# One PSUM bank per output row: product laid, rectified in place, y accumulated on it

## The chip, the cores and the metric

The kernel runs on one core of one Trainium2 chip. The metric is device time in microseconds (us). The kernel before was recorded at 440.18 us (median of 3 runs, 438.61 to 440.63). All times compared below are of fast runs unless a line says otherwise (a run counts as slow when it is over 1.5% above the fastest of the same kernel in its call).

## The reference

```python
scores = q @ k.T / sqrt(64), causal, window of 64 keys        # 8 batches, 8 heads, 576 rows
x = softmax(scores) @ v                                       # [8, 576, 512]
X = rfft(x, axis=1)[:, :64]                                   # 64 modes
Y = X * (w_r + i w_i)        # a 512 x 512 complex matrix for each mode
y = irfft(Y, n=576, axis=1)
u = x + y
out = u + relu(u @ w_ch)
```

The weights are 64 x 2 matrices of 512 x 512 in float32: 162 MB are read from HBM in all. `u @ w_ch` is computed as `x @ w_ch` (called Z here) plus the inverse transform of `Y @ w_ch`.

## The kernel before

There are three stages. The attention stage ends near 145 us; TensorE, ACT and DVE share it, and GpSimd issues the loads of weights as buffers come free. The mode stage follows the weight stream: mode after mode, 32 small matmuls each. Modes 0 to 47 (the 96 "early" rows of the spectrum) are folded into Z while the last 16 modes stream in. The tail starts when the last weight lands: the 32 "late" rows (modes 48 to 63) are transposed and multiplied with `w_ch` ("turn", once for each four batches), then 36 output row tiles are made. A row tile is 128 rows of one batch, or for `t = NT - 1` a pair of 64-row remainders of two batches.

The tail before, with two PSUM banks for each row (`psc` for the channel product, `psu` for y):

```python
def group(h, todo, folds, ...):                 # four rows at a time
    for b, t in todo:                           # Z into psc by an identity matmul
        nc.tensor.matmul(out=psc, lhsT=ident_r, rhs=channel_out(...), start=True, stop=False)
    for b, t, pair, psc in ts:                  # late rows, 32 of 128 contraction rows
        nc.tensor.matmul(out=psc, lhsT=trigL[pp, ...], rhs=Ywl[h][pp, :], start=False, stop=True)
    for i, (b, t, pair, psc) in enumerate(ts):
        fold = i in folds                       # x by a matmul, for about half of the rows
        ...                                     # if fold: psu = x_sb
        nc.tensor.matmul(out=psu, lhsT=trigI[...], rhs=Yb[...], ...)        # y
        nc.scalar.activation(out=r, in_=psc, func=Relu)
        if fold: nc.vector.tensor_tensor(out=ot, in0=psu, in1=r, op=add)
        else:    nc.vector.tensor_tensor(out=ot, in0=psu, in1=x_sb[...], op=add)
                 nc.gpsimd.tensor_tensor(out=ot, in0=ot, in1=r, op=add)
        nc.sync.dma_start(out=out[...], in_=ot)
```

A mode's matmuls, real and imaginary in turn for each of four output blocks `e`, and the eviction of eight modes at once by DVE and ACT:

```python
for e in range(NC):
    for c in range(NC): matmul(psy[:, m % MG, e, :], wr[...], XQ[...])
    if e == 0: between()
    for c in range(NC): matmul(psy[:, m % MG, e, :], wi[...], XQ[...])
...
if m % MG == MG - 1:
    for ri in range(2): evac(YT or YTl, psy, ri)     # DVE, then ACT
```

The softmax here doesn't subtract the row's maximum and nothing guards it: scores larger than these inputs give would overflow.

## Time and profile before

| | before |
|---|---|
| runs | 438.61, 440.18, 440.63 us |
| span of the profiled run | 438.7 us (that run: 440.46 us) |
| last imaginary matmuls start | 391.91 us |
| first late row | 397.60 us |
| last result in SBUF | 432.10 us |
| busy in the span: PE, DVE, ACT, POOL | 76%, 44%, 34%, 26% |

The times in the table are read from the list of instructions in order of time (start us, us, engine, line, operation, out<-in, count). Busy shares over the whole span say little here: they average an attention stage, a mode stage, and the tail. The prediction below shows the lines and how they were read.

This is ACT in the attention stage, in order of time (start us, us, engine, line, operation, out<-in, count):

```profile
51.70 1.74 ACT L58 COPY kT<-pst 128x768 bf16<-128x768 bf16 x2
53.33 1.09 ACT L292 ACTIVATE et<-pss 128x512 bf16<-128x512 f32 x2
```

### The profile page before, as it was taken

What the parts mean: (1) busy time and instruction counts of PE and PEld (TensorE: products, weight loads), DVE (VectorE), ACT (ScalarE), POOL (GpSimd) and SP (SyncE); (2) the same over time, 40 slices, a digit from 0 to 9 for tenths busy, and PEclk for the clock granted to TensorE, in tenths of its full rate; (3) what the DMA queues carried; (4) which work ended last, traced back from release to release, by engine and by line L of the source; (5) the groups of instructions that cost most, each with busy time, mean ns of one, the idle gap of its engine ahead of it and who ended that gap; (6) DMA issues with size and microseconds to landing.
All of it is one profiled execution on the core that took longest, in us unless ns stands there. A gap on an engine that the chain in (4) does not pass through costs nothing. (4 is left out here: it accounts for less than half of the span.)

```text
span 438.7 us, 11675 instructions
## 1 busy us (share of the span) xinstructions
PE 333.5 (76%) x5152; PEld 226.8 (52%) x5152; DVE 191.1 (44%) x384; ACT 147.4 (34%) x261; POOL 112.1 (26%) x188
## 2 busy tenths in 40 slices
PE   6999999989988864222388888986458666989991
PEld 2465666656654763112266676764335344555550
DVE  5465766666754004028522232222133433336772
ACT  4476866767753001001022232322001010105561
POOL 7131322231022232121122122221021212105473
PEclk9999999999998555555567898689585675899998
DMA  7999999999999999999999999999999999942685
GB/s 143 211 214 213 212 212 214 211 214 214 214 213 198 214 213 259 214 213 213 214 214 212 214 214 213 216 211 214 214 213 214 214 213 213 214 97 109 235 314 207
DMA packets 30643, 91.98 MB, mean 210 GB/s; under 512 B 3072, under 2 KB 3072, under 8 KB 30592
## 3 DMA queue, kind: packets, MB, share of 16 engines
q0 software_dynamic: 25344, 81.80, 93.6%
q1 hardware_dynamic: 5248, 9.44, 6.0%
q8 instruction: 40, 0.66, 0.5%
q14 instruction: 11, 0.09, 0.1%
HBM read 162.53 MB, written 9.44 MB: 392 GB/s over the span
## 5 line engine op out<-in xcount | busy, mean ns | idle before, releaser
L511 PE MATMUL psy<-XQ,wt 128*128 128x16 bf16 x880 | 54.9, 191 | 49.3 <-DMA wt<-in_moe_w_i_dram 47.9
L506 PE MATMUL psy<-XQ,wt 128*128 128x16 bf16 x912 | 57.2, 191 | 27.7 <-DMA wt<-in_moe_w_r_dram 27.1
L511 PEld LDWEIGHTS <-wt 128*128 128x128 bf16 x880 | 42.8, 104 | 59.9 <-DMA wt<-in_moe_w_i_dram 55.9
L506 PEld LDWEIGHTS <-wt 128*128 128x128 bf16 x912 | 43.1, 103 | 38.1 <-DMA wt<-in_moe_w_r_dram 34.5
L117 POOL DMA_DIRECT2D wt<-in_moe_w_i_dram x55 | 29.4, 535 | 125.9 <-PE psy L511 59.6
L541 DVE CAST xT<-pxt 128x512 fp32r<-128x512 bf16 x36 | 23.2, 686 | 64.9 <-PE pxt L538 64.9
L544 PE MATMUL psz<-wch,xT 128*128 128x512 f32 x144 | 48.8, 489 | 0.1
L117 POOL DMA_DIRECT2D wt<-in_moe_w_r_dram x57 | 30.7, 538 | 63.7 <-DMA wt<-in_moe_w_r_dram 35.3
L546 ACT CAST Z<-psz 128x512 fp32r<-128x512 f32 x36 | 21.1, 587 | 72.3 <-PE psz L544 72.3
L292 ACT ACTIVATE et<-pss 128x512 bf16<-128x512 f32 x72 | 39.2, 599 | 12.6 <-PE pss L286 12.5
L662 DVE TENSOR_TENSOR Z<-pse,Z 128x512 fp32r<-128x512 f32 x36 | 23.7, 688 | 33.6 <-PE pse L642 33.6
L310 PE MATMUL pso<-vt,et 128*64 128x65 bf16 (+1 forms) x576 | 32.6, 204 | 4.1 <-DVE x_sb L318 4.0
L544 PEld LDWEIGHTS psz<-wch,xT 128*128 128x128 f32 x144 | 31.9, 234 | 6.6 <-issue 0.2
L310 PEld LDWEIGHTS <-et 128*64 128x64 bf16 (+1 forms) x576 | 22.3, 109 | 15.6 <-issue 7.6
L751 POOL TENSOR_TENSOR ot<-ot,r 128x512 f32<-128x512 f32 x18 | 22.8, 1286 | 29.1 <-ACT Yb L58 24.0
L318 DVE TENSOR_TENSOR x_sb<-pso,rcp 128x640 bf16<-128x640 f32 x32 | 26.3, 822 | 0.9
L59 DVE CAST YT<-psy 128x256 fp32r<-128x256 f32 x6 | 2.5, 421 | 47.8 <-PE psy L511 47.8
L744 ACT ACTIVATE r<-psc 128x512 f32<-128x512 f32 x36 | 19.0, 601 | 10.3 <-PE psc L729 9.7
L267 PE MATMUL pss<-band,ident_bf 64*64 64x512 bf16 x160 | 20.6, 391 | 1.6 <-ACT et L292 1.6
L59 DVE COPY vT<-pst 128x768 bf16<-128x768 bf16 x16 | 15.3, 958 | 13.4 <-PE pst L213 13.4
L642 PE MATMUL pse<-yw,trigI 96*128 96x512 f32 x40 | 19.9, 566 | 0.0
L656 ACT CAST yw<-psw 96x512 fp32r<-96x512 f32 x8 | 4.7, 583 | 44.8 <-PE psw L653 44.8
(160 smaller groups left out, 532.5 us busy)
## 6 DMA issues: line engine op xcount, KB each, us to landing
wt<-in_moe_w_r_dram POOLq DMA_DIRECT2D x57, 512.0 KB, 19.1
wt<-in_moe_w_i_dram POOLq DMA_DIRECT2D x55, 512.0 KB, 19.1
out_dram<-ot SPq DMA_DIRECT2D x32, 256.0 KB, 2.2
rk<-in_k_dram POOLq DMA_DIRECT2D x8, 576.0 KB, 10.0
rq<-in_q_dram POOLq DMA_DIRECT2D x8, 576.0 KB, 13.8
rv<-in_v_dram POOLq DMA_DIRECT2D x8, 576.0 KB, 12.6
kT<-in_moe_w_i_dram POOLq DMA_DIRECT2D x2, 512.0 KB, 8.2
qT<-in_moe_w_r_dram POOLq DMA_DIRECT2D x2, 512.0 KB, 9.9
```

Of the source, the lines that this page charges most:

```text
L117: nc.gpsimd.dma_start(out=wt, in_=src[m].rearrange("(p c) e -> p c e", c=NC))
L267: nc.tensor.matmul(out=pss[(2 * w + hh) % 3][64 * half:64 * half + 64, :], lhsT=ident_bf[pp, pp], rhs=view(band[pp], 128 * half, [[0, WIN ...
L292: nc.scalar.activation(out=et[:, hh, :], in_=pss[(2 * w + hh) % 3], func=ACT_F.Exp, scale=EX_SCALE)
L310: nc.tensor.matmul(out=pso[po, hh, (i // 2) * VW:(i // 2) * VW + D + 1], lhsT=et[pk, hh, col:col + 64], rhs=vt[pk, 1 - f % 2, 2 * hh + g / ...
L318: nc.vector.tensor_tensor(out=view(x_sb, b * NT * DM + g * D, [[4 * D, 2], [DM, NT], [1, D]]), in0=view(pso, 0, [[512, 2], [VW, NT], [1, D]]),
L506: nc.tensor.matmul(out=psy[:, m % MG, e, :], lhsT=wr[:, c, ee], rhs=XQ[:, c, :, 1:3, m], start=(c == 0), stop=(m == 0 and c == NC - 1))
L511: nc.tensor.matmul(out=psy[:, m % MG, e, :], lhsT=wi[:, c, ee], rhs=XQ[:, c, :, 0:2, m], start=False, stop=(c == NC - 1))
L541: nc.vector.tensor_copy(out=xT, in_=pst)
L544: nc.tensor.matmul(out=psz, lhsT=xT[:, c, :], rhs=wch[:, c, :], start=(c == 0), stop=(c == NC - 1))
L546: nc.scalar.copy(out=channel_out(i), in_=psz)
L662: nc.vector.tensor_tensor(out=channel_out(i), in0=ps, in1=channel_out(i), op=ALU.add)
L751: nc.gpsimd.tensor_tensor(out=ot, in0=ot, in1=r, op=ALU.add)
```

## The change

The intent: a row keeps one PSUM bank. The identity matmul lays Z, the late rows are added, ACT rectifies the bank in place, y is accumulated on the rectified value, and one DVE add with x gives the result. GpSimd's adds and the x matmuls go. So that one table serves, late rows are placed by batch at partitions 96 to 127 of zero-padded tiles (`Ywm`, `Yb`), by GpSimd copies. The last mode gets its own bank: all its real matmuls, and the first four products, run before its imaginary weight lands. For the pair rows, x of the second batch is copied to partitions 64 to 127 of the first one's tile.

```diff
-    trigL = late2.tile([128, S + 64], FP32R, name="trigL")
...
-        if m % MG == 0:
+        if m % MG == 0 or m == NM - 1:
             psy = ps_y.tile([128, MG, NC, 2 * B], FP32, name="psy")
...                                     # in the building of the table trigI
-                    nc.vector.tensor_scalar(out=trigL[:, 576:640], ...)
+                for b in range(0, B, 2):
+                    nc.scalar.copy(out=x_sb[64:128, b, NT - 1, :], in_=x_sb[0:64, b + 1, NT - 1, :])
...                                     # last mode
+            for e in range(NC):
+                for c in range(NC):
+                    real(e, c)
+            between()                   # [z_row(i) for i in range(NR)] + [idle(6)]
             for c in range(NC):
+                for e in range(NC):
+                    imag(e, c)
...                                     # tail, NR = 4 and two more banks, LA = 2
+    def l_row(i):
+            nc.tensor.matmul(out=banks[i], lhsT=trigI[:, tr:tr + 128], rhs=Ywm[bb % NM2], start=False, ...)
+        nc.scalar.activation(out=banks[i], in_=banks[i], func=ACT_F.Relu)
+    def u_row(i):
+            nc.tensor.matmul(out=banks[i], lhsT=trigI[:, tr:tr + 128], rhs=Yb[bb // 2][:, bb % 2, :], start=False, ...)
+        nc.vector.tensor_tensor(out=ot, in0=banks.pop(i), in1=x_sb[...], op=ALU.add)
+        nc.sync.dma_start(...)
+        for i in range(len(order) + LA):
+            if i < len(order):
+                if i >= NR: z_row(i)
+                l_row(i)
+            if i >= LA: u_row(i - LA)
```

More of the change, by code (lines that the diff above doesn't have):

```diff
@@ L476 @@
     trigI = late2.tile([128, S + 128], FP32R, name="trigI")
-    trigL = late2.tile([128, S + 64], FP32R, name="trigL")
     Z0 = late2.tile([128, len(tiles), DM], FP32R, name="Z0")
-    p2d = ExitStack()
+    p2d = ctx.enter_context(ExitStack())
     ps_a = p2d.enter_context(tc.tile_pool(name="ps_a", bufs=1, space=PSUM, reuse_waits="tile"))
@@ L500, in mode, with real, imag @@
         wr, wi = wtiles.pop((m, 0)), wtiles.pop((m, 1), None)
-        if m % MG == 0:
+        if m % MG == 0 or m == NM - 1:
             psy = ps_y.tile([128, MG, NC, 2 * B], FP32, name="psy")
-        for e in range(NC):
-            ee = slice(128 * e, 128 * e + 128)
-            for c in range(NC):
-                nc.tensor.matmul(out=psy[:, m % MG, e, :], lhsT=wr[:, c, ee],
-                                 rhs=XQ[:, c, :, 1:3, m], start=(c == 0), stop=(m == 0 and c == NC - 1))
-            if e == 0:
-                between()
-            for c in range(NC if m else 0):
-                nc.tensor.matmul(out=psy[:, m % MG, e, :], lhsT=wi[:, c, ee],
-                                 rhs=XQ[:, c, :, 0:2, m], start=False, stop=(c == NC - 1))
+        def real(e, c):
+            nc.tensor.matmul(out=psy[:, m % MG, e, :], lhsT=wr[:, c, 128 * e:128 * e + 128],
+                             rhs=XQ[:, c, :, 1:3, m], start=(c == 0 and (m < NM - 1 or e == 0)),
+                             stop=(m == 0 and c == NC - 1), skip_group_check=True)
+        def imag(e, c):
+            nc.tensor.matmul(out=psy[:, m % MG, e, :], lhsT=wi[:, c, 128 * e:128 * e + 128],
+                             rhs=XQ[:, c, :, 0:2, m], start=False, stop=(c == NC - 1),
+                             skip_group_check=True)
+        if m < NM - 1:
+            for e in range(NC):
+                for c in range(NC):
+                    real(e, c)
+                if e == 0:
+                    between()
+                for c in range(NC if m else 0):
+                    imag(e, c)
+        else:
+            for e in range(NC):
+                for c in range(NC):
+                    real(e, c)
+            between()
+            for c in range(NC):
+                for e in range(NC):
+                    imag(e, c)
         while nw < NLOAD:
@@ L519, in mode @@
             nw += 1
-        if m % MG == MG - 1:
+        if m % MG == MG - 1 or m == NM - 2:
             g = m // MG
+            m0 = m % MG if m == NM - 1 else 0
+            n1 = m % MG + 1 - m0
             dst, n, g = (YT, E0, g) if g < L0 else (YTl, 128 - E0, g - L0)
-            for ri in range(2):
-                evac(view(dst, g * 2 * MG + ri * MG, [[B * n, NC], [n, B], [1, MG]]),
-                     view(psy, ri, [[2 * B, NC], [2, B], [NC * 2 * B, MG]]), ri)
+            if m < NM - 1:
+                for ri in range(2):
+                    evac(view(dst, g * 2 * MG + ri * MG, [[B * n, NC], [n, B], [1, n1]]),
+                         view(psy, ri, [[2 * B, NC], [2, B], [NC * 2 * B, n1]]), ri)
+            else:
+                evac(view(dst, g * 2 * MG + m0, [[B * n, NC], [n, B], [MG, 2]]),
+                     view(psy, m0 * NC * 2 * B, [[2 * B, NC], [2, B], [1, 2]]), False)
     with ExitStack() as p2a:
@@ L582, in floor @@
                         return f
-                    f32 = floor(32, pcol, "f32")
-                    f64 = floor(64, pcol, "f64")
-                    lcol, odd, even = col("lcol"), col("odd"), col("even")
-                    nc.vector.scalar_tensor_tensor(out=lcol, in0=f32, scalar=-32.0, in1=pcol,
-                                                   op0=ALU.mult, op1=ALU.add)
-                    nc.vector.tensor_single_scalar(out=lcol, in_=lcol, scalar=float(E0), op=ALU.add)
-                    nc.vector.scalar_tensor_tensor(out=odd, in0=f64, scalar=-2.0, in1=f32,
-                                                   op0=ALU.mult, op1=ALU.add)
-                    nc.vector.tensor_scalar(out=even, in0=odd, scalar1=-1.0, scalar2=1.0,
-                                            op0=ALU.mult, op1=ALU.add)
-                    for tab, row in ((trigI, pcol), (trigL, lcol)):
+                    for tab, row in ((trigI, pcol),):
                         fa, fb = floor(2 * MG, row, "fa"), floor(MG, row, "fb")
@@ L617 @@
                             nc.vector.tensor_scalar(out=tis, in0=tis, scalar1=coefs, scalar2=None, op0=ALU.mult)
-                            o2 = 576 if tab is trigI else 512
+                            o2 = 576
                             for c0, c1, o in ((0, SW, i * SW),) if i < 3 else ((0, 80, 432), (80, SW, o2)):
@@ L625 @@
                                             scalar2=None, op0=ALU.mult)
-                    nc.vector.tensor_scalar(out=trigL[:, 576:640], in0=trigL[:, 512:576], scalar1=odd,
-                                            scalar2=None, op0=ALU.mult)
-                    nc.vector.tensor_scalar(out=trigL[:, 512:576], in0=trigL[:, 512:576], scalar1=even,
-                                            scalar2=None, op0=ALU.mult)
+                for b in range(0, B, 2):
+                    nc.scalar.copy(out=x_sb[64:128, b, NT - 1, :], in_=x_sb[0:64, b + 1, NT - 1, :])
     yw = wmid.tile([128, 2, DM], FP32R, name="yw", tag="wm")
@@ L643, in early_rows, with z_row @@
                              start=start and r0 == 0, stop=stop and r0 + n == 128)
+    p3 = ctx.enter_context(ExitStack())
+    NM2 = 3
+    ywmp = p3.enter_context(tc.tile_pool(name="ywmp", bufs=1, side="right", reuse_waits="tile"))
+    Ywm = [ywmp.tile([128, DM], FP32R, name=f"Ywm{i}") for i in range(NM2)]
+    for t_ in Ywm:
+        nc.vector.tensor_scalar(out=t_[:E0], in0=trigI[:E0, 0:DM], scalar1=0.0, scalar2=None,
+                                op0=ALU.mult)
+    NR = 4
+    ps_e = p3.enter_context(tc.tile_pool(name="ps_e", bufs=NR, side="right", space=PSUM, reuse_waits="tile"))
+    order = []
+    for b in range(0, B, 2):
+        order += [(b, t) for t in range(NT - 1)] + [(b + 1, 0), (b, NT - 1)]
+        order += [(b + 1, t) for t in range(1, NT - 1)]
+    banks = {}
+    def z_row(i):
+        if i % (NR + 2) < NR:
+            banks[i] = ps_e.tile([128, DM], FP32, name="row", tag="pse")
+        else:
+            banks[i] = ps_f.tile([128, DM], FP32, name="rowf")
+        nc.tensor.matmul(out=banks[i], lhsT=ident_r, rhs=channel_out(tiles.index(order[i])),
+                         start=True, stop=False, skip_group_check=True)
     with ExitStack() as p2c:
-        ps_e = p2c.enter_context(tc.tile_pool(name="ps_e", bufs=3, space=PSUM, reuse_waits="tile"))
         def spectrum(b):
@@ L668, in idle @@
         def idle(n):
-            psd = ps_e.tile([128, DM], FP32, name="psd", tag="pse")
+            psd = ps_a.tile([128, DM], FP32, name="psd", tag="psa")
             for _ in range(n):
@@ L683 @@
             for m in range(L0 * MG, NM):
-                mode(m, lambda: some(1, m))
                 if m < NM - 1:
+                    mode(m, lambda: some(1, m))
                     some(2 if m % 8 != 7 else 1, m)
@@ L688 @@
                     assert not work
-                    idle(4)
+                    mode(m, lambda: [z_row(i) for i in range(NR)] + [idle(6)])
     p2b.close()
-    p2d.close()
     wl.close()
-    with ExitStack() as p3:
-        yp = p3.enter_context(tc.tile_pool(name="yp", bufs=1, reuse_waits="tile"))
-        tp = p3.enter_context(tc.tile_pool(name="tp", bufs=5, reuse_waits="tile"))
-        op = p3.enter_context(tc.tile_pool(name="op", bufs=11, reuse_waits="tile"))
-        ps_u = p3.enter_context(tc.tile_pool(name="ps_u", bufs=4, space=PSUM, reuse_waits="tile"))
-        ps_c = p3.enter_context(tc.tile_pool(name="ps_c", bufs=4, space=PSUM, reuse_waits="tile"))
-        R = 128 - E0
-        def turn(h):
-            psa = ps_u.tile([128, NC, 128], FP32R, name="psl", tag="psu")
-            psw = ps_c.tile([128, DM], FP32, name="pslw", tag="psc")
-            yl = [view(YTl, (e * B + 4 * h) * R, [[1, 128]]) for e in range(NC)]
-            for e in range(NC):
-                nc.tensor.transpose(out=psa[:, e, :], in_=yl[e], identity=ident_r)
-            for e in range(NC):
-                nc.tensor.matmul(out=psw, lhsT=yl[e], rhs=wch[:, e, :],
-                                 start=(e == 0), stop=(e == NC - 1))
-            for bb in range(4):
-                evac(Yb[2 * h + bb // 2][E0:128, bb % 2, :],
-                     psa[R * bb:R * bb + R].rearrange("p c e -> p (c e)"), bb == 3)
-                if bb == 2:
-                    nc.scalar.copy(out=Ywl[h], in_=psw)
-        def group(h, todo, folds, between=lambda: None):
-            ts = []
-            for b, t in todo:
-                psc = ps_c.tile([128, DM], FP32, name="psc", tag="psc")
-                nc.tensor.matmul(out=psc, lhsT=ident_r, rhs=channel_out(tiles.index((b, t))),
-                                 start=True, stop=False)
-                ts.append((b, t, t == NT - 1, psc))
-            between()
-            for b, t, pair, psc in ts:
-                pp = slice(R * (b - 4 * h), R * (b - 4 * h) + (2 * R if pair else R))
-                nc.tensor.matmul(out=psc, lhsT=trigL[pp, 128 * t:128 * t + 128], rhs=Ywl[h][pp, :],
-                                 start=False, stop=True)
-            for i, (b, t, pair, psc) in enumerate(ts):
-                fold = i in folds
-                psu = ps_u.tile([128, DM], FP32, name="psu", tag="psu")
-                if fold:
-                    for bb, r0, n in parts_of(b, t):
-                        nc.tensor.matmul(out=psu[r0:r0 + n, :], lhsT=ident_bf[:n, :n],
-                                         rhs=view(x_sb[:n], (bb * NT + t) * DM, [[1, DM]]),
-                                         start=True, stop=False)
-                for bb, r0, n in parts_of(b, t):
-                    tr = 128 * t + (64 - r0 if pair else 0)
-                    nc.tensor.matmul(out=psu, lhsT=trigI[:, tr:tr + 128], rhs=Yb[bb // 2][:, bb % 2, :],
-                                     start=not fold, stop=(r0 + n == 128))
-                r = tp.tile([128, DM], FP32, name="r")
-                nc.scalar.activation(out=r, in_=psc, func=ACT_F.Relu)
-                ot = op.tile([128, DM], FP32, name="ot")
-                if fold:
-                    nc.vector.tensor_tensor(out=ot, in0=psu, in1=r, op=ALU.add)
-                else:
-                    nc.vector.tensor_tensor(out=ot, in0=psu,
-                                            in1=view(x_sb, (b * NT + t) * DM, [[1, DM]]), op=ALU.add)
-                    nc.gpsimd.tensor_tensor(out=ot, in0=ot, in1=r, op=ALU.add)
-                for bb, r0, n in parts_of(b, t):
-                    nc.sync.dma_start(out=out[bb, 128 * t:128 * t + n, :], in_=ot[r0:r0 + n, :])
-        Ywl = [yp.tile([128, DM], FP32R, name=f"Ywl{h}") for h in range(2)]
-        with tc.manual_schedule(engines={mybir.EngineType.PE}):
-            turn(0)
-            for h in range(2):
-                bs = range(4 * h, 4 * h + 4)
-                for t in range(NT - 1):
-                    group(h, [(b, t) for b in bs], (1, 3) if t else (3,))
-                    if t == 1:
-                        group(h, [(4 * h, NT - 1), (4 * h + 2, NT - 1)], (0, 1))
-                        if h == 0:
-                            turn(1)
@@ new lines, with turn @@
+    R = 128 - E0
+    yp = p3.enter_context(tc.tile_pool(name="yp", bufs=1, reuse_waits="tile"))
+    op = p3.enter_context(tc.tile_pool(name="op", bufs=10, reuse_waits="tile"))
+    ps_f = p3.enter_context(tc.tile_pool(name="ps_f", bufs=2, space=PSUM, reuse_waits="tile"))
+    Ywl = [yp.tile([128, DM], FP32R, name=f"Ywl{h}") for h in range(2)]
+    Yl = [yp.tile([128, DM], FP32R, name=f"Yl{h}") for h in range(2)]
+    def turn(h):
+        psw = ps_a.tile([128, DM], FP32, name="psw")
+        psa = ps_a.tile([128, NC, 128], FP32R, name="psa", tag="psa")
+        yl = [view(YTl, (e * B + 4 * h) * R, [[1, 128]]) for e in range(NC)]
+        for e in range(NC):
+            nc.tensor.matmul(out=psw, lhsT=yl[e], rhs=wch[:, e, :],
+                             start=(e == 0), stop=(e == NC - 1))
+        for e in range(NC):
+            nc.tensor.transpose(out=psa[:, e, :], in_=yl[e], identity=ident_r)
+        flat = psa.rearrange("p c e -> p (c e)")
+        if h == 0:
+            nc.scalar.copy(out=Ywm[0][E0:128], in_=psw[0:R])
+            nc.vector.tensor_copy(out=Yb[0][E0:128, 0, :], in_=flat[0:R])
+        nc.scalar.copy(out=Ywl[h], in_=psw)
+        nc.vector.tensor_copy(out=Yl[h], in_=flat)
@@ new lines, in place_w, with place_y, cols @@
+    def place_w(b):
+        h, j = divmod(b, 4)
+        if b:
+            nc.gpsimd.tensor_copy(out=Ywm[b % NM2][E0:128], in_=Ywl[h][R * j:R * j + R])
+    def place_y(b):
+        h, j = divmod(b, 4)
+        if b:
+            nc.gpsimd.tensor_copy(out=Yb[b // 2][E0:128, b % 2, :], in_=Yl[h][R * j:R * j + R])
+    def cols(b, t):
+        return [(bb, 128 * t + (64 - r0 if t == NT - 1 else 0)) for bb, r0, n in parts_of(b, t)]
+    def l_row(i):
+        b, t = order[i]
+        cs = cols(b, t)
+        for bb, tr in cs:
+            nc.tensor.matmul(out=banks[i], lhsT=trigI[:, tr:tr + 128], rhs=Ywm[bb % NM2],
+                             start=False, stop=(bb == cs[-1][0]), skip_group_check=True)
+        nc.scalar.activation(out=banks[i], in_=banks[i], func=ACT_F.Relu)
@@ new lines, in u_row @@
+    def u_row(i):
+        b, t = order[i]
+        cs = cols(b, t)
+        for bb, tr in cs:
+            nc.tensor.matmul(out=banks[i], lhsT=trigI[:, tr:tr + 128], rhs=Yb[bb // 2][:, bb % 2, :],
+                             start=False, stop=(bb == cs[-1][0]), skip_group_check=True)
+        ot = op.tile([128, DM], FP32, name="ot")
+        nc.vector.tensor_tensor(out=ot, in0=banks.pop(i), in1=view(x_sb, (b * NT + t) * DM, [[1, DM]]),
+                                op=ALU.add)
+        for bb, r0, n in parts_of(b, t):
+            nc.sync.dma_start(out=out[bb, 128 * t:128 * t + n, :], in_=ot[r0:r0 + n, :])
@@ new lines @@
+    LA = 2
+    with tc.manual_schedule(engines={mybir.EngineType.PE, mybir.EngineType.Activation,
+                                     mybir.EngineType.DVE, mybir.EngineType.Pool}):
+        turn(0)
+        for b in range(4):
+            if b < NM2:
+                place_w(b)
+            place_y(b)
+        for i in range(len(order) + LA):
+            if i < len(order):
+                if i >= NR:
+                    z_row(i)
+                l_row(i)
+            if i >= LA:
+                u_row(i - LA)
+            if i < len(order):
+                done = {5: 0, 8: 1}.get(i % 9)
+                if done is not None:
+                    b = 2 * (i // 9) + done + NM2
+                    if b < B:
+                        place_w(b)
+            if i == 5:
+                turn(1)
+                for b in range(4, B):
+                    place_y(b)
```

## The prediction

> **What bounds the kernel now.** The metric is 440.18 us (438.61 to 440.63); the profiled execution has a span of 438.7 us. I read the forty slices first, to split the run into stages.
>
> ```profile
> PE   6999999989988864222388888986458666989991
> PEclk9999999999998555555567898689585675899998
> DMA  7999999999999999999999999999999999942685
> GB/s 143 211 214 213 212 212 214 211 214 214 214 213 198 214 213 259 214 213 213 214 214 212 214 214 213 216 211 214 214 213 214 214 213 213 214 97 109 235 314 207
> ```
>
> The transfers fill slices 1 to 34 (about 11 to 384 us) at a steady 214 GB/s: the weight stream. Whatever the engines do there is hidden, so an operation that the change adds or removes before the last weight lands is worth nothing. Only what follows counts. The chain of waits gives the seam and the end:
>
> ```profile
> 379.67 12.19 DMA wt<-in_moe_w_i_dram
> ...
> 391.91 0.29 PE psy L511 x4
> ...
> 428.74 0.37 DVE ot L749
> 429.10 0.45 issue
> 429.57 1.18 POOL ot L751
> 430.81 1.29 POOLq L791
> ```
>
> The last weight lands at 391.86; the tail from there to 438.7 is 46.8 us. Next, the tail by stretches (columns: busy us and count of PE, PEld, DVE, ACT, POOL, then clock, DMA share, GB/s):
>
> ```profile
> 390.40:393.80 3.40, 2.01 (x33) 1.12 (x32) 0.42 (x1) 0.37 (x1) 0.00 (x0) 0.97 0.02 4
> 393.80:397.20 3.40, 3.38 (x11) 2.79 (x12) 2.06 (x3) 0.59 (x1) 0.00 (x0) 0.53 0.00 0
> ```
>
> The first late transposes and channel products run at half clock (0.53). In steady state (411.0 to 428.3) TensorE reads 17.30 of 17.30 us busy, and the transfers only 272 GB/s. That is not TensorE at its peak, as the list in order of time shows:
>
> ```profile
> 417.47 1.45 PE L723 MATMUL psc<-Z,ident_r 128*128 128x512 f32 x4
> 418.85 0.50 PE L729 MATMUL psc<-Ywl,trigL 32*128 32x512 f32 x4
> 419.28 0.49 PE L741 MATMUL psu<-Yb,trigI 128*128 128x512 f32 x1
> ```
>
> Four identity matmuls take 1.38 us start to start where unhindered they take 0.93 (the group at 423.83 in the chain): they wait for banks that the rectifier still reads. Four rows come in bursts, all products, all late rows, then all y. The groups of instructions in the tail give the durations:
>
> ```profile
> L751 POOL TENSOR_TENSOR ot<-ot,r 128x512 f32<-128x512 f32 x18 | 22.8, 1286 | 29.1 <-ACT Yb L58 24.0 <-DVE ot L749 3.2 <-ACT r L744 1.0
> L744 ACT ACTIVATE r<-psc 128x512 f32<-128x512 f32 x36 | 19.0, 601 | 10.3 <-PE psc L729 9.7 <-POOL ot L751 0.6
> L741 PE MATMUL psu<-Yb,trigI 128*128 128x512 f32 x40 | 16.0, 492 | 0.0
> L723 PE MATMUL psc<-Z,ident_r 128*128 128x512 f32 x36 | 12.4, 435 | 0.0
> L749 DVE TENSOR_TENSOR ot<-psu,x_sb 128x512 f32<-128x512 f32 x18 | 12.0, 685 | 6.2 <-PE psu L741 6.2
> L736 PE MATMUL psu<-x_sb,ident_bf 128*128 128x512 bf16 x14 | 5.4, 388 | 0.5 <-ACT Yb L58 0.4
> ```
>
> Single durations contain the pipeline's fill. The spacing of back-to-back ones is what counts for a rate. It is 0.233 us for a full fp32r matmul (0.93 for four), 0.49 for ACT's rectifier (2.07 us for four, less one 0.60, over three), 0.60 for DVE's add (starts at 426.34, 426.94, 427.54).
>
> **What the Trainium skill says.** (1) "PSUM — Partial Sum Buffer", The four PSUM rules: ScalarE's writes leave the has-written bits alone, so y accumulates on a rectified value if a matmul wrote the element before. The identity matmul does, so the sum should be right; no accumulation of this kind is in the trace before. (2) "TensorE: Matmul & The Clock Gate", Part 3: matmuls of 32 rows in different row groups run together. The trace agrees: the four late matmuls above take 0.43 us start to start, 0.108 each against 0.233 for full ones. Padding them to 128 rows gives that up. (3) Same page, Part 1: the clock follows activity over windows of some 3.4 us. The trace agrees: a stretch of 3.40 us with 2.01 us of mostly 16-column matmuls and idle time is followed by 3.4 us at 0.53. (4) "GPSIMD Engine Reference", 3.1: [...] 512 elements, 769 ns measured at best, a two-input add about 2.6 cycles an element. This trace has the add at 1286 ns; it has no such copy, so my 0.9 us for one with its start cost is an estimate from that page.
>
> **The change, part by part.**
>
> Hidden: the second table (some 7 us of DVE work between 204 and 214 us) goes, four ACT copies and three zero fills come, all under the weight stream. Worth 0. The last weight should land at 391.9 again.
>
> Last mode: before, 4 imaginary and 24 further matmuls followed the landing, 0.98 us. Now all 16 real ones and four products are done earlier and only 16 imaginary follow: at 0.115 us per four (the spacing of such groups at 392) plus fill, 0.63. Its eviction is 64 elements on DVE instead of 256 on DVE and 256 on ACT (0.42 and 0.37, in series): estimate 0.22. So the first channel product starts at 391.91 + 0.63 + 0.30 = 392.84, where the late transposes started at 393.82. The wait before the landing is filled: reals 0.5, products 0.93, six idle matmuls 1.3, from 388.96 to about 391.7, where before TensorE stood for 1.4 us. I expect the clock to stay near 1.0, so the four products take the 1.16 us of the second turn (406.55), not 2.03.
>
> First late row: products done at 394.0, ACT's 32-row copy 0.58, late row issued at 394.65. It was at 397.60. ACT then copies the rest (+0.49), and rectifies the first row at 395.05 to 395.65. First y at 395.65, after some 0.35 us of waiting, first add from 396.05 to 396.75, first store issued at 396.8, against 400.72.
>
> TensorE's sum from there: 36 rows need 36 products, 40 late matmuls and 40 y; four products and three late ones are behind us. 109 x 0.233 = 25.4 us, plus 1.3 for the second turn (406.25 to 407.55), = 26.7: last y issued at 422.35, plus about 0.4 waiting for the last rectifier = 422.75. What is saved in matmuls is small: 22 folded x_sb matmuls go (14 full at 0.215, 8 half, about 4.3 us in all), but the late ones cost 40 x 0.233 = 9.3 instead of about 36 x 0.108 = 3.9. The gain is in the waits between bursts: two banks per row become one of six, three row slots ahead, so that nothing waits longer than a row.
>
> End: fill 0.38, add 0.69, last result at 423.8 against 432.1 (the last GpSimd add starts at 430.8): 8.3 us. If the last store drains as before (6.6 us from last result to end), span 430.4; without its backlog up to 0.7 less. The early start gives about 2.9, the 0.8 or so per row becoming 0.69 the rest.
>
> **Rivals.** (a) Another engine becomes the bound. Per row TensorE 0.70 (with pairs 0.72), DVE 0.60, ACT 0.49. DVE has 36 adds and three copies, 23.4 us in 27; close, not over. If jitter makes each row 0.05 longer, +1.8 us.
> (b) The stores become the bound. Peak rate in the tail is 387 GB/s (405 to 406 us), so 262 KB take 0.68 us and all 9.44 MB 24.6 us. From 397.4 that is 422.0 at the earliest: equal to TensorE's pace. It can't lengthen the end by more than about 1 us, but a faster TensorE could not gain more than that either.
> (c) GpSimd's 14 copies. Needed: the second batch's late rows at 396.6, about 1.5 us after their source. At 0.9 us it holds; at 2 us or more the y copies delay later late rows and the gain shrinks to 3 us or less.
> (d) ACT reading and writing one bank is slow. Nothing in the trace shows such an instruction. If its spacing doubled to 1 us, 36 us for the rows would eat the gain.
> (e) The clock falls again at 394 to 397: about +1.5 us.
>
> **The range.** The centre sum is span 430.4. The runs' median reads 1.5 us above the span of the profile (440.18 against 438.7): 431.9, or 431.2 without the backlog. Rivals (a), (c), (d), (e) only add, a shorter fp32r spacing (0.225) would take off 0.9. I say 431.3, 428.8 to 435.5. The 2% line lies at 431.4, right at the centre: faster 0.46, same 0.51, slower 0.03.
>
> **What would show it.** Right: last weight near 391.9, first rectifier near 395.1, clock near 1.0 at 394, rectifier near 0.6 us in place, stores above 340 GB/s for 25 us, last add near 423.8. Wrong: a row period set by ACT or DVE (TensorE's products idle, released by the add), GpSimd as releaser of late rows, clock 0.5 in the first turn, or a seam later than 392.5.

## The result

Four runs of the changed kernel took 435.75 to 436.12 us, median 435.98; the four of the kernel before 438.61 to 440.63, median 439.54. The ratio is 0.9918, 95% interval 0.9890 to 0.9945. (A ratio is the mean time of one kernel's fast runs over that of the other's of the same rounds, so it is not quite the ratio of the medians.) The change is faster by 0.8%, less than the 2% at which the record calls a kernel faster, so its class there is "same"; the prediction had 431.3 us with a range from 428.8 to 435.5. The outputs are correct.

The profiled run took 436.12 us, span 434.3. Its slices:

```profile
PE   6899999999999676322787878873265857799994
PEclk9999999996996755555788977896555756599999
DMA  8999999999999799999999999999999999992698
GB/s 143 211 213 212 214 212 213 212 213 214 213 204 194 132 214 213 260 213 214 213 214 214 213 214 214 212 214 214 213 214 214 214 213 214 213 214 51 236 338 300
```

Slices 12 to 14 (about 119 to 152 us) moved 204, 194 and 132 GB/s. The kernel before has 213, 198 and 214 in its slices of those numbers. The weight stream lost nearly five microseconds' worth more there than in the kernel before, ahead of the mode stage. Next the seam and the end, from the chain of waits:

```profile
397.23 0.49 PE psy L509 x16
397.74 0.28 DVE YTl L59
398.15 1.18 PE psw L737 x4
399.36 0.57 ACT Ywm L743
...
428.29 0.68 DVE ot L776
428.97 0.60 DVEq L832
```

The imaginary matmuls of the last mode start at 397.07 and not near 391.9. This is the group's line in the list in order of time:

```profile
397.07 0.64 PE L509 MATMUL psy<-XQ,wt 128*128 128x16 bf16 x16
```

From there on everything is short: eviction 0.28, products, one 32-row copy, first late row at 399.98, last result at 428.97. The groups of the tail (`row` are four of the six banks; the lines of the other two, `rowf`, are alike):

```profile
L776 DVE TENSOR_TENSOR ot<-row,x_sb 128x512 f32<-128x512 f32 x24 | 16.4, 691 | 2.1 <-PE row L773 2.0
L767 ACT ACTIVATE row<-row 128x512 f32<-128x512 f32 x24 | 13.7, 583 | 3.4 <-PE row L765 0.9 <-DVE ot L776 0.7
L773 PE MATMUL row<-Yb,trigI 128*128 128x512 f32 x26 | 10.1, 401 | 0.2 <-ACT row L767 0.2
L765 PE MATMUL row<-Ywm,trigI 128*128 128x512 f32 x26 | 9.7, 397 | 0.4 <-ACT Ywm L743 0.4
L756 POOL CAST Yb<-Yl 32x512 fp32r<-32x512 f32 x7 | 4.3, 613 | 1.7 <-DVE Yl L746 1.5
```

In place, ACT takes 583 ns where it took 601. TensorE's groups have next to no idle time before them: the bursts are gone. GpSimd's copies take 613 ns.

Put together (before, after, difference; all from the two profiled runs):

| stretch | before | after | difference |
|---|---|---|---|
| start to last imaginary matmuls | 391.91 | 397.07 | +5.16 |
| from there to the first late row | 5.69 | 2.91 | -2.78 |
| first late row to last result | 34.50 | 28.99 | -5.51 |
| last result to end | 6.6 | 5.3 | -1.3 |
| span | 438.7 | 434.3 | -4.4 |

So the tail gave 9.6 us and the stages before it took 5.2 back. ACT in the attention stage shows where that begins; this is the same place as the two lines of the kernel before:

```profile
51.12 0.83 ACT L58 COPY kT<-pst 128x768 bf16<-128x768 bf16 x1
52.23 0.62 ACT L639 COPY x_sb<-x_sb 64x512 bf16<-64x512 bf16 x1 [0.27 <-DVE x_sb L318]
52.87 0.81 ACT L58 COPY kT<-pst 128x768 bf16<-128x768 bf16 x1
53.57 1.09 ACT L292 ACTIVATE et<-pss 128x512 bf16<-128x512 f32 x2
```

The pair-row copy stands in the program among the code that builds the table, at mode 15. But ACT's order was left to the scheduler in that part, and the copy needs nothing except x, so it was moved up to the moment when x is there: between two evictions. ACT waits 0.27 for x, copies for 0.62, and the next exponential comes 0.24 later than in the kernel before where all earlier ones had come 0.57 to 0.58 earlier, a shift of 0.8. TensorE now waits for that exponential, which it did not do at this place before:

```profile
54.23 0.40 PE L267 MATMUL pss<-band,ident_bf 64*64 64x512 bf16 x2 [0.25 <-ACT et L292]
```

The second copy, at 83.6 us, shifts by 0.8 at first and 0.65 lastingly, the third, at 117.6, likewise. In between, the clock of TensorE was at 0.50 for some seven microseconds (about 99 to 106) in the changed kernel and at 1.00 in the other, which cost 2.6 more. A stretch of 2.50 us inside it, before and then after (columns as in the prediction: PE, PEld, DVE, ACT, POOL, clock, DMA share, GB/s), with 53 matmuls and 35:

```profile
100.00:102.50 2.50, 2.50 (x53) 1.56 (x52) 1.79 (x3) 1.76 (x4) 0.53 (x1) 1.00 1.09 215
```
```profile
100.00:102.50 2.50, 2.50 (x35) 1.60 (x33) 1.59 (x2) 1.04 (x2) 0.00 (x0) 0.50 1.08 214
```

When the stage's last buffers come free, GpSimd issues the loads into them; before, and then after:

```profile
139.19 0.53 POOL L117 DMA_DIRECT2D kT<-in_moe_w_i_dram  x1 [8.33 <-issue]
```
```profile
144.23 0.53 POOL L117 DMA_DIRECT2D kT<-in_moe_w_i_dram  x1 [9.38 <-issue]
```

That is 5.0 us later. The view names no releaser for this load; the next one, 2.14 us later in both kernels, waits for TensorE's `pso`. By then the earlier loads had run dry (3 GB/s between 142.5 and 145.0 us), and the stream, at its full rate of some 213 GB/s from there on, did not catch up.

My theory after this: the copies, moved into the attention stage, delay the weights, by their own time and perhaps by the half clock. The rivals: that other parts of the change make the seam late (PSUM pools, zero-filled tiles, the order of the last mode); that the half clock comes by chance; and that the six idle matmuls overran the landing.

### The profile page after: what moved, and what is told of

It reads as the page before. It is cut to its first block, busy times and chain, and to the rows that moved or that the text cites. A ratio compares the mean times of both kernels' runs of the same rounds, so it can differ in the third digit from the quotient of the medians.

```text
span 434.3 us, 11554 instructions
## 1 busy us (share of the span) xinstructions
PE 331.8 (76%) x5131; PEld 230.4 (53%) x5131; DVE 181.8 (42%) x335; ACT 148.8 (34%) x256; POOL 97.9 (23%) x184
## 3 DMA queue, kind: packets, MB, share of 16 engines
q1 hardware_dynamic: 5248, 9.44, 6.1%
HBM read 162.53 MB, written 9.44 MB: 396 GB/s over the span
## 4 chain that ended last, share of the span: by engine, by line
DMA 45%; PE 36%; DVE 8%; issue 5%; ACT 4%; POOL 1%; DVEq 0%; POOLq 0%; ACTq 0%
DMA wt<-in_moe_w_r_dram 24%; DMA wt<-in_moe_w_i_dram 21%; PE pso L310 6%; PE pst L213 5%; PE psv L230 3%; DVE x_sb L318 3%; PE psx L332 2%; PE pss L267 2%; PE pss L365 2%; PE psd L704 2%; DVE vT L59 2%; PE pss L286 2%; PE psy L509 2%; ACT vt L58 1%; PE psy L504 1%
## 5 line engine op out<-in xcount | busy, mean ns | idle before, releaser
L566 PE MATMUL psz<-wch,xT 128*128 128x512 f32 x144 | 47.8, 474 | 0.0
L566 PEld LDWEIGHTS psz<-wch,xT 128*128 128x128 f32 x144 | 29.8, 223 | 5.4
L267 PE MATMUL pss<-band,ident_bf 64*64 64x512 bf16 x160 | 22.7, 421 | 2.1 <-ACT et L292 2.1
L58 ACT CAST YT<-psy 128x256 fp32r<-128x256 f32 x6 | 2.2, 374 | 59.8 <-DVE YT L59 52.5
L776 DVE TENSOR_TENSOR ot<-row,x_sb 128x512 f32<-128x512 f32 x24 | 16.4, 691 | 2.1 <-PE row L773 2.0
```

What stands on the lines that cost most here:

```text
L267: nc.tensor.matmul(out=pss[(2 * w + hh) % 3][64 * half:64 * half + 64, :], lhsT=ident_bf[pp, pp], rhs=view(band[pp], 128 * half, [[0, WIN ...
L566: nc.tensor.matmul(out=psz, lhsT=xT[:, c, :], rhs=wch[:, c, :], start=(c == 0), stop=(c == NC - 1))
```

## The experiments

Eleven kernels ran, in three calls; each call has its own runs of the kernel before on the same chip (medians 439.11, 439.14 and 438.96 us). All outputs were correct.

### Copies held back (e1_late)

```diff
-                for b in range(0, B, 2):
-                    nc.scalar.copy(out=x_sb[64:128, b, NT - 1, :], in_=x_sb[0:64, b + 1, NT - 1, :])
+                    one = col("one")
+                    nc.vector.tensor_single_scalar(out=one, in_=trigI[:, 0:1], scalar=-1.0e9, op=ALU.is_ge)
+                    for b in range(0, B, 2):
+                        nc.scalar.activation(out=x_sb[64:128, b, NT - 1, :], in_=x_sb[0:64, b + 1, NT - 1, :],
+                                             func=ACT_F.Copy, scale=one[0:64])
```

The factor is always 1.0; it only makes the copies wait for the table. They then ran at 177 to 180 us.

> The changed kernel with its four ACT copies of the pair rows held back behind the building of the table (each is multiplied by a 1.0 that is computed there), so that ACT's order in the attention stage is that of the kernel before. Theory (the copies, moved into the attention stage, make the weight stream start late): the last imaginary matmuls start at 392.0 to 392.5 instead of 397.07, the tail of 37.2 us stays, span 429.3 to 429.8, time about 431 us, ratio to the kernel before 0.980 to 0.982. Rival (the late seam comes from the PSUM pools, the zero-filled tiles or the order of the last mode): seam still near 397, time about 436.

Measured: 430.50 to 434.97, median 431.50; ratio 0.9822 (0.9777 to 0.9868). The median is as the theory said. The profiled run, 432.95 us, was one of the slower ones: TensorE at half clock from about 130 to 137 us, imaginary matmuls at 394.53 and span 431.2, so in this profile the theory's 392.0 to 392.5 and 429.3 to 429.8 were missed. The runs fall into steps: three near 430.7, then 432.2, 432.95 and 434.97. The kernel before does the same (seven runs of 438.6 to 439.2, two near 440.5, two near 443). So a single profile can mislead by two or more microseconds, and the next runs were compared by their whole sets.

### The copies alone on the kernel before (e2_before_copies)

```diff
                     nc.vector.tensor_scalar(out=trigL[:, 512:576], in0=trigL[:, 512:576], scalar1=even,
                                             scalar2=None, op0=ALU.mult)
+                for b in range(0, B, 2):
+                    nc.scalar.copy(out=x_sb[64:128, b, NT - 1, :], in_=x_sb[0:64, b + 1, NT - 1, :])
```

> The kernel before with nothing but the four ACT copies of the pair rows added at the place where the change has them (nothing reads them, the result stays right). Theory: the attention stage ends about 5 us later, the last weight lands 4 to 5 us later, time 443.5 to 445 us, ratio 1.009 to 1.012. Rival (copies are hidden, something else in the change delays the weights): 439.5 us, ratio 1.000.

Measured: 441.89 to 443.56, median 442.44, ratio 1.0066 (1.0023 to 1.0109). Four copies that nothing reads cost 3.3 us by medians, and 3.3 between the fastest runs (441.89 against 438.61). Less than I had expected, but the sign and the cause are clear, and the rival that expected 439.5 is out. In its profile the clock was at 1.00 from 97.5 to 105 us, so the half clock there is not needed for the loss; the last imaginary matmuls started at 394.96, and a part of the tail that the kernel before had at half clock ran at full clock (below).

### Two of the copies (e3_before_last_two)

```diff
-                for b in range(0, B, 2):
+                for b in (4, 6):
```

> The kernel before with only the copies for batches 4 and 6 (in the attention stage at about 117 and 147 us). In the changed kernel the first two copies cost 0.65 us each, and then TensorE ran at half clock from 98.9 to 105.5, which cost 2.6 more. Theory A (the half clock comes from the shift of 0.7 us that the first copies make): no half clock at 99 to 105, attention ends 0.8 to 2 us later, time 440 to 441.5. Theory B (each copy costs alike, about 1.2 us of seam): about 442. Theory C (the half clock at 99 is chance): it can show here as well, then 442.5 to 444.

Measured: 438.69, 440.67, 440.87, 441.02; ratio 1.0011 (0.9961 to 1.0060). No half clock at 99 to 105. The median, 440.77, lies in theory A's range, but one run is as fast as the kernel before, and against the steps in the kernel before this set of four cannot tell a cost of 0.8 us from none. Inconclusive.

### Without the idle matmuls (e4_no_idle)

```diff
-                    mode(m, lambda: [z_row(i) for i in range(NR)] + [idle(6)])
+                    mode(m, lambda: [z_row(i) for i in range(NR)])
```

> The changed kernel without the six idle matmuls ahead of the last imaginary ones. In its trace TensorE had no idle time there: products and idle matmuls ran to 396.97, so the weight may have landed earlier. Theory A (idle matmuls overran the landing): the imaginary matmuls start 0.3 to 0.8 us earlier, time about 435.5, unless the clock falls. Theory B (the landing was at 397 anyway): start unchanged. If the clock falls to 0.5 in the following turn, +1.5 us: about 437.

Measured: 435.01 to 436.00, median 435.26, ratio 0.9898 (0.9852 to 0.9945). The order of time shows both effects that had been set against each other:

```profile
395.02 0.65 PE L509 MATMUL psy<-XQ,wt 128*128 128x16 bf16 x16 [0.67 <-DMA wt<-in_moe_w_i_dram]
...
397.95 1.65 PE L765 MATMUL row<-Ywm,trigI 128*128 128x512 f32 x3 [0.36 <-ACT Ywm L743]
```

TensorE now waits 0.67 for the weight, and the clock falls: the first three late rows take 1.65 us, against 0.96 in the changed kernel. The imaginary matmuls start 2.05 us earlier than in the changed kernel's profile, more than theory A's 0.3 to 0.8; the half clock near 99 us is missing, so that is not the idle matmuls' doing alone. By medians the gain is 0.7 us, but the sets are from different calls, and the changed kernel's second set (e5, 434.84) is as fast: no gain is shown. As in e2, the clock at 97.5 to 105 was 1.00 here with all copies in place.

### The changed kernel again (e5_after_again)

No edit.

> The changed kernel once more, unedited, on the same chip as the next three, because single runs of one kernel fall into steps of about 2 us (the kernel before: 438.6 to 443.5) with the stretches in which TensorE's clock is halved in the attention stage. Theory (the copies in the attention stage cost the seam some 4 us on average): about 435.9, 4 to 5 us above the version with held-back copies (430.5 to 435.0, median 431.5). Rival (the difference of the first series was the clock's chance): medians within 1.5 us of each other.

Measured: 433.04 to 435.69, median 434.84, ratio 0.9879 (0.9834 to 0.9924). It is 3.3 us above e1_late and 3.8 above e6_late_idle3 (of the same call) by medians: less than 4 to 5, but more than the rival allowed. The two sets of this one kernel differ by 1.1 us in their medians. The profiled run (435.69), the slowest of the six, again had the half clock from 98 to 106 us and the imaginary matmuls at 397.23.

### Held-back copies, three idle matmuls (e6_late_idle3)

```diff
-                    mode(m, lambda: [z_row(i) for i in range(NR)] + [idle(6)])
+                    mode(m, lambda: [z_row(i) for i in range(NR)] + [idle(3)])
```

(on top of e1_late)

> The held-back copies with three idle matmuls instead of six ahead of the last imaginary ones. In the run with six, TensorE came from the idle matmuls to the imaginary ones at 394.53 without waiting for the weight, whose transfers had ended at 393.0 (in the kernel before the landing followed the end of transfers by 1.1 us). Theory: landing at about 394.1 in such a run, gain 0.3 to 0.6 us, median about 431. Rival (clock falls as in the run without any idle matmul, where three late rows took 1.65 instead of 0.96 us): no gain.

Measured: 429.97 to 434.90, median 431.02, ratio 0.9810 (0.9759 to 0.9861). The profiled run (430.53) has the imaginary matmuls at 391.47 without a wait, and the clock holds (0.96 for three late rows):

```profile
391.47 0.64 PE L509 MATMUL psy<-XQ,wt 128*128 128x16 bf16 x16
...
394.39 0.96 PE L768 MATMUL row<-Ywm,trigI 128*128 128x512 f32 x3 [0.38 <-ACT Ywm L746]
```

The gain of 0.5 us is in the expected range and inside the spread of the runs; it is not shown by these numbers.

### Last mode in its old order (e7_old_last_mode)

```diff
-        if m < NM - 1:                  # real and imaginary in turn
+        if m < NM:
...
-                    mode(m, lambda: [z_row(i) for i in range(NR)] + [idle(6)])
+                    mode(m, lambda: some(1, m))
+                    idle(4)
...
-                if i >= NR:
-                    z_row(i)
+                z_row(i)
```

(on top of e1_late)

> The held-back copies, but the last mode in its old order (real and imaginary interleaved, idle matmuls as before) and the first four products in the tail. Theory: 0.35 us more between landing and eviction and up to 0.93 for four products, about 1.3 us in all, plus up to 1.3 more if the clock is at 0.5 in the first turn as in the kernel before: median 432.5 to 434. Rival (those matmuls fit into waits for ACT's copy anyway): within 0.5 us of the held-back version.

Measured: 430.36 to 432.57, median 430.74, ratio 0.9805 (0.9742 to 0.9868). The rival won: the early real matmuls and the early products are worth nothing that these runs show.

```profile
391.20 0.29 PE L509 MATMUL psy<-XQ,wt 128*128 128x16 bf16 x4 [0.74 <-DMA wt<-in_moe_w_i_dram]
...
394.12 0.47 PE L678 MATMUL row<-Z,ident_r 128*128 128x512 f32 x1
394.65 0.50 PE L769 MATMUL row<-Ywm,trigI 128*128 128x512 f32 x1
394.98 0.40 PE L678 MATMUL row<-Z,ident_r 128*128 128x512 f32 x1
```

From the imaginary matmuls to the first late row it takes 3.45 us where e6 takes 2.92, but the products lie in the wait for ACT's 32-row copy and rectifier, and in the old order the imaginary matmuls start when the weight lands (after a wait of 0.74), not when the products and idle matmuls are through. From the imaginary matmuls to the end: 428.6 - 391.20 = 37.4 us here, 428.7 - 391.47 = 37.2 in e6.

### Four banks (e8_four_banks)

```diff
-        if i % (NR + 2) < NR:
-            banks[i] = ps_e.tile([128, DM], FP32, name="row", tag="pse")
-        else:
-            banks[i] = ps_f.tile([128, DM], FP32, name="rowf")
+        banks[i] = ps_e.tile([128, DM], FP32, name="row", tag="pse")
```

(on top of e1_late)

> The held-back copies with four PSUM banks for the rows instead of six. Theory (the tail runs at TensorE's pace because a bank is free in time): with four, a product waits for the add of the row four before it. Product to y is 8 matmuls of 0.233, fill and add 1.1 more: period 0.83 instead of 0.70 us, 32 rows, about 4 us slower: 435 to 436. Rival (TensorE or the stores set the pace whatever the banks): within 1 us of the held-back version.

Measured: 435.05 to 436.05, median 435.84, ratio 0.9904 (0.9851 to 0.9957), 4.3 us above e1_late; expected were about 4. The list of waits in the tail names the releaser:

```profile
PEld row L675 <- DVE ot L776: 9.1, 26, 0.6
```

TensorE waited 26 times, 9.1 us in all, for the add that frees a bank. From the imaginary matmuls (391.75) to the end it took 433.3 - 391.75 = 41.5 us, against 37.2. So the tail runs at TensorE's pace with six banks and not with four.

### Added band products (e9_filler and e11_before_filler)

```diff
-                mask(w + 1, max(1, 3 - n))
+                mask(w + 1, max(1, 5 - n))
```

(e9 on top of e6_late_idle3, e11 on the kernel before)

> The version with held-back copies and three idle matmuls, and in the attention stage up to two more repeats of the band product in each window that has little else to do (five less the number of queued pieces, where it was three), so that TensorE stands less in the waits of 0.5 and 0.6 us before the half clock near 130 us. Theory (the half clock there follows from those waits and costs the seam 1.5 to 2 us where it lasts two windows): no half clock between 128 and 140 us, or a shorter one, runs closer together, median 429.5 to 430.5. Rival (the added products only lengthen the stage, the clock falls all the same): 432 or more.

> The kernel before with the added band products alone, to tell what they do without the change. Theory (they hold the clock in the attention stage): median 437.5 to 438.7, and none of the runs above 441. Rival (they only lengthen the stage): 440 or more.

Measured: e9 434.91 to 438.57, median 435.69, ratio 0.9916; e11 442.22 to 444.07, median 443.63, ratio 1.0076 (1.0034 to 1.0117). Both theories failed; the rivals had the times right and the clock wrong. The clock did stay at 1.00 from 100 to 140 us in both profiles (that of e9, the slowest of its six runs, had a half clock at about 87 to 90 us), but the added matmuls cost about 4.7 us in either kernel (435.69 - 431.02, from two calls, and 443.63 - 438.96). Whether a steady clock alone would bring the runs together stays open. What the pair does show is that TensorE's time in the attention stage passes into the end of the program, with or without the change, as ACT's did.

### Copies on GpSimd (e10_pool_copies)

```diff
-                    nc.scalar.copy(out=x_sb[64:128, b, NT - 1, :], in_=x_sb[0:64, b + 1, NT - 1, :])
+                    nc.gpsimd.tensor_copy(out=x_sb[64:128, b, NT - 1, :], in_=x_sb[0:64, b + 1, NT - 1, :])
```

> The changed kernel with the four pair-row copies on GpSimd instead of ACT, at the same place in the program; they run early as well, but ACT's order in the attention stage is then that of the kernel before. Theory (it is ACT's time in the attention stage that delays the weights): as with held-back copies, median 430.5 to 432. Rival (the copies do harm on any engine, here by holding up the loads that GpSimd issues): 434 to 436.

Measured: fast runs 430.23, 430.27, 430.75, 430.82 and 432.85, a sixth of 439.14 left out (slow by the 1.5% rule; its clock of 0.803 is not lower than the 0.802 of the 432.85 run); median of all six 430.78, ratio 0.9801 (0.9751 to 0.9851). The copies still run early:

```profile
52.38 0.60 POOL L639 COPY x_sb<-x_sb 64x512 bf16<-64x512 bf16 x1 [4.35 <-DVE x_sb L318]
```

With the copies off ACT, and nothing else edited, the imaginary matmuls start at 391.82 and the span is 428.5:

```profile
391.82 0.64 PE L509 MATMUL psy<-XQ,wt 128*128 128x16 bf16 x16
```

So it is the copies' place on ACT, not the copies, that the changed kernel paid for. This edit of one line beats both kernels by medians, as do e1, e6 and e7 (whether by 2% of the kernel before is unclear for all four); the runs do not rank these four.

## Why the prediction was wrong, point by point

**The step that failed** is the paragraph "Hidden": "four ACT copies and three zero fills come, all under the weight stream. Worth 0. The last weight should land at 391.9 again." The copies are not at mode 15, where the program has them, but in the attention stage, in front of work that TensorE waits for. With the copies on ACT the imaginary matmuls started at 397.07 and 397.23 in two profiles; with them on GpSimd at 391.82, and held back at 394.53 and 391.47. These profiles overstate it: the changed kernel's two were the slowest runs of their sets, those with the copies on GpSimd and with e6's edit among the faster. By medians the copies cost 3.3 us on the kernel before (e2) and 3.3 to 4.1 in the changed kernel (e5 against e1, e6 and e10). I had also reasoned that under a saturated weight stream nothing counts. A stream is only saturated as long as loads are issued in time, and the issue followed TensorE and ACT: the four copies alone moved the load of 139.19 us to 143.23 (e2), the added band products moved it to 144.62 (e11). The slices did show a dip there in the kernel before (198 GB/s in slice 13), which I passed over. With the copies off ACT (e10) the median, 430.78, is near my 431.3.

The thirteen profiles show how far such a delay carries. Where that load was issued at 139.7 us or earlier (the kernel before, e6, e7, e8, e10; the earliest at 137.23), the weight transfers ended between 390.5 and 391 us. Where it was issued at 140.75 (e3), 141.11 (e1), 142.75 (e4), 143.23 (e2) and 144.23 (the changed kernel), they ended near 391.7, 392.7, 393.8, 394.3 and 395.3; e5, e9 and e11 follow the same line. So a delay passed on nearly whole and an advance of up to 2 us gained nothing; what sets that limit was not tested.

**What of the 5.2 us is not settled.** Three copies before the end of the attention stage shift it by about 0.65 us each, 1.9 to 2.0 together. The load came 5.0 us later, and the changed kernel had been 0.6 ahead before the first copy, so 5.6 were lost. The rest of that is half clock: 2.6 at 99 to 106 us and 1.1 near 130, where the kernel before has a shorter stretch of it too. The half clock at 99 occurred in both profiles of the changed kernel and in neither e2 nor e4, which have the same copies, nor in any of the profiles without the first two. That the copies' shift makes it likelier is possible, and these runs don't decide it.

**The tail** was right nearly to the number. Counted from the imaginary matmuls, I had 2.74 us to the first late row, then 29.15 to the last result; measured were 2.91 and 28.99. Shifted by the 5.16 of the seam, my 423.8 for the last result becomes 428.96; it was 428.97. That the two misses cancel to 0.01 us is luck. The bound was as foreseen: a row took 0.70 us of three matmuls at 0.233, and DVE and ACT kept up. (Rival (a)'s 0.72 with pairs should read 0.75, 116 matmuls over 36 rows; the sum used the right count.) e8 shows that the number of banks matters: two fewer cost 4.3 us with the same matmuls. That the gain is not one of fewer matmuls rests on the prediction's count, in which the padded late rows cost more than the folded ones saved. What GpSimd's adds or the padding are worth by themselves no run shows.

**The last mode and the early products** were put at about 1 us from the landing on, and TensorE's sum counted four products as behind it. e7 shows no gain: the products fit in the wait for ACT, and with six idle matmuls, 1.3 us, TensorE reached the imaginary matmuls later than the weight allowed: without them it waited only 0.67 (e4).

**The clock in the first turn.** I expected near 1.0 and it was, but I put the half clock of the kernel before (the products there took 2.03 us) down to its program. In e2 and e3, with the tail of the kernel before, they took 1.16 and 1.15 at clock 1.00, and from the imaginary matmuls to the end they needed 45.6 us where the profiled run of the kernel before needed 46.8. So some 1.2 us of my gain was not in the change but in that profiled run.

That half clock went with TensorE's idle time. In every profile, take the 3.4 us near the seam (386 to 410 us) in which TensorE was least busy. In the kernel before they are 390.4 to 393.8, with 2.0 us busy because TensorE waited 1.38 for the last weight, and in e4 394.4 to 397.8, with 2.1. In these two the clock fell to 0.50 as that stretch ended and stayed there for some 3.4 us. In the other eleven the least was 2.4 us or more, and the clock held. In the attention stage the same measure does not sort the cases (the clock held after stretches with 2.34 and fell after some with 2.6), so this is an observation at the seam and not a rule.

**Rivals.** (a), (c), (d), (e) did not occur: GpSimd's copies took 613 ns instead of my 900, and ACT's in-place rectifier 583. (b), the stores: they ran behind, as allowed for, at 306 GB/s from 402 to 429 us and not above the 340 that I had named as a sign (and 9.44 MB at 387 GB/s are 24.4 us, not my 24.6). The last result was ready at 428.97 and the transfers went on until about 432.7. Yet from last result to end took 5.3 and not 6.6 us, because the program ended 1.5 us after the last transfer, where the kernel before needed 4.25. SyncE there waited up to 2.5 us for TensorE's sequencer in the closing barrier; after the change 0.5. Why, I did not test.

Put right in these terms, the sum is: predicted span 430.4, seam +5.2, end -1.3, measured 434.3. The -1.3 was luck: the one thing that I had named as shortening the end, a missing backlog of stores, did not come about.

## What to carry to other kernels

"Hidden under the stream" is a statement about where an instruction runs, so look at the engine's order after scheduling, not at the line in the source: an operation with early inputs moves up, and on an engine that others wait for it can cost more than its own time (here each 0.62 us copy cost 0.65, and in the two profiles of the changed kernel a half clock followed). A load stream that is full on average still depends on whoever frees its buffers; here a delay of 5.0 us there reached the seam as 5.2. And where runs of one kernel come in steps, compare sets of runs before believing the differences of two profiles.

## What the Trainium skill lacked or had wrong

- "GPSIMD Engine Reference", 3.1: it gives no time for a copy. Its 769 ns for 512 elements are the best case of a tight loop, and I took them for a copy's. Here 14 copies of 32x512 fp32r took 612 to 613 ns, and the 64x512 bf16 ones 605 (e10). My 0.9 us, worked out from the page, was half as much again.
- "PSUM — Partial Sum Buffer", The four PSUM rules: accumulating on a value that ScalarE wrote works where a matmul had set the bits, as the page says; the outputs are correct in every run. What it lacks is a figure for ScalarE reading and writing one bank: 583 ns for 128x512, against 601 ns into SBUF.
- "TensorE: Matmul & The Clock Gate", Part 1: it does not say how far a partly busy window may go before the clock falls. At the seam, with 2.0 and 2.1 us busy of 3.4, it fell, and with 2.4 or more it held, in thirteen profiles; in the attention stage no such line can be drawn.
